# Sigmoid attention and a gated feed-forward layer on one Trainium2 core: output tiles summed in PSUM over three pairs of feed-forward tiles, weight sums rounded on GpSimd, stores issued later, first operands loaded sooner

## The chip, the cores and the metric

The program runs on one core of one Trainium2 chip. The time is that of the device in microseconds (us). The kernel before took 1407.16 us in the median of three runs (1405.22 to 1414.54). Engines are named as in the profile: PE is TensorE (matmul), PEld its weight load, DVE VectorE, ACT ScalarE, POOL GpSimd, and SP SyncE, which here issues every DMA.

## The reference

Twelve heads of 64 in a batch of 8 with 448 positions; the attention's 3584 x 768 output goes through a gated layer with 1536 hidden columns.

```python
scores = scale * np.matmul(q, k.transpose(0, 1, 3, 2)) - np.log(S)
attn = 1.0 / (1.0 + np.exp(-scores))
x = np.matmul(attn, v)                 # then (B*S, H*D) = (3584, 768)
gate = 1.0 / (1.0 + np.exp(-(x @ w_gate)))
val = x @ w_val
return gate * val @ w_out
```

q, k and v are float32; the three weights reach the kernel as 64-bit words, of which VectorE makes two float32 words (hi and lo) by shifts and masks.

## The kernel before, in words

**Stage 1, attention.** 24 steps `m` (8 batches x 3 groups of four heads) of 7 beats `g` each, 168 beats in all. A beat is four matmul calls `scores` (L227), which the profile shows as 8 records, the sigmoid of their result on ACT (L230), and two beats later the `values` matmuls (L244), 8 records too. Score tiles have two buffers in PSUM, so PE's scores wait for ACT's sigmoid of two beats before. When a head pair is done, ACT copies one PSUM half (L254) and DVE adds the other (L261); the sum `x` is stored to DRAM (`xd`).

**The weights.** `Words.first` and `Words.second` (L105 to L125) turn one 128 x 384 chunk of 64-bit words into `t` (hi) and `a`, with eight DVE instructions for a whole chunk (L109 to L112, L122 to L124, L128). `convert` (L130) makes of the chunks what the matmuls need. For a pair `jp` of feed-forward tiles and for gate and value (`t` of the loop), four chunks are a 2 x 2 block; a product of two blocks is made from 7 instead of 8 matmul groups, and for that 7 operands are stored per block: three chunks and four sums of chunks. Each operand is a tile `whl` (hi and lo), stored to `ad` (`store`, L134). The output weights (`wo`, four chunks per pair) are split only and stored to `od` (L169). `convert` is a generator of 32 steps per pair; a chunk takes two steps, a sum one. The weights of the first three pairs (set 0) are converted beside the attention (96 steps over 160 beats), those of the last three (set 1) beside the feed-forward of set 0, where `tick` (L472) advances the generator after every product and every output tile, 96 steps over 280 ticks.

**The pool.** Beside the attention the generator's tiles lie in the pool `att` with two buffers each, beside the feed-forward in `ff` with one buffer each: there `wa` and `wt` of a chunk can be written only when the stores of the chunk before have landed.

**Stage 2, feed-forward.** Eight visits: 2 sets x 4 pairs of batches. In a visit each of three pairs `jp` takes two units of 7 products: gate, then value (`hidden`). A product is 9 matmuls (3 chunks x 3 terms hi and lo, L362) into one of four PSUM banks `un`; ACT or DVE takes it out. A unit's sums run on DVE and two of them on POOL (L373). `hidden` multiplies by the gate and splits the result into `hh` (ACT) and `hl` (DVE). Then come the output tiles: 12 per pair (2 batches x 6 blocks `o`), each 6 matmuls (L442) into one of four banks `mm`, which ACT or DVE adds to a tile `sum` in SBUF (L446, L449, L451). The 36 tiles of a visit stand between its units. The last pair's `sum` goes to DRAM: as `part` in set 0, and as output in set 1, whose first pair adds the loaded `part` (`pb`).

**The next visit's operands.** `load_x` (L176) loads 12 tiles `x`; `split_x` (L183) makes 21 operands `bh`, `bl` of them: 12 subtractions on POOL (L192), 21 roundings on ACT (L196), 21 differences on DVE (L197). For visit 0 this runs beside the attention (from step 8 on), for the others between the last 18 output tiles of a visit, one or two per tile.

**What sets the order.** It is written out by hand: each engine takes its instructions in the order of the program. SP has one queue for all DMAs; an issue that waits holds up those behind it. Operands `A` come through a ring of 7 (`load_operand`, called after each product, waits for that product's matmuls), `wo` through a ring of 8 (`load_out`).

## Time and profile before

| | |
|---|---|
| runs | 1405.22, 1407.16, 1414.54 us |
| the profiled execution | 1409.0 us, its span 1407.2 us |
| busy | PE 1284.3, PEld 1019.8, DVE 840.2, ACT 467.9, POOL 447.6 us |
| mean granted TensorE clock | 0.96 |
| DMA | 341.13 MB, 242 GB/s over the span, 72.2% of 16 engines' time |

Read first which engine the span hangs on, then stage by stage what PE waits for. The busy time of PE counts matmuls that overlap each other and those at a lower clock, so a busy PE is not PE at its peak: the distance from one matmul to the next in a stretch without waits is the measure.

### The profile page before, as it was taken

Reading aid. Unit: us, or ns where it says so; the run is one execution under the profiler, and the core shown is the slowest. Engines: PE = TensorE matmul, PEld = TensorE weight load, DVE = VectorE, ACT = ScalarE, POOL = GpSimd, SP = SyncE. Lnnn points to the kernel's source line nnn. Section 1 sums busy time; section 2 is a strip of 40 time slices with the busy share of each in tenths; the row PEclk is TensorE's granted clock in tenths of the full one; section 3 lists DMA queues with packets and bytes.
Section 4 is the critical chain, followed back from the end, with each engine's and each line's share of the span. In section 5 each row is a group of like instructions: output and inputs, shape, how many; then the busy total and the mean of one; then the engine's idle time right before and its main releaser. Section 6 shows DMA issues by size and latency. Waiting matters only on the chain.

```text
span 1407.2 us, 20966 instructions
## 1 busy us (share of the span) xinstructions
PE 1284.3 (91%) x7456; PEld 1019.8 (72%) x7456; DVE 840.2 (60%) x1466; ACT 467.9 (33%) x769; POOL 447.6 (32%) x388
## 2 busy tenths in 40 slices
PE   8998899979978997799889798999999989989998
PEld 3333333458967986689778796988798878978897
DVE  5575686535678668766785458344734563465445
ACT  6676677732222322222222213212221231122120
POOL 3313523114362344522544124213422332252121
PEclk9999999999999999899989999999899999999999
DMA  8989688878857985596658865875587568747763
GB/s 281 324 279 339 206 311 309 280 271 302 278 183 271 321 281 181 191 359 212 237 195 306 271 194 172 273 255 169 184 292 224 152 207 274 241 124 237 209 194 109
DMA packets 159559, 341.13 MB, mean 242 GB/s; under 512 B 16352, under 2 KB 71776, under 8 KB 159456
## 3 DMA queue, kind: packets, MB, share of 16 engines
q1 hardware_dynamic: 159456, 339.80, 72.2%
q8 instruction: 59, 0.97, 0.3%
q14 instruction: 44, 0.36, 0.1%
HBM read 264.24 MB, written 75.50 MB: 241 GB/s over the span
## 4 chain that ended last, share of the span: by engine, by line
PE 51%; DVE 8%; POOL 8%; DMA 8%; issue 6%; ACT 1%; SPq 0%; POOLq 0%; DVEq 0%; ACTq 0%
PE un L362 35%; PE acc L442 14%; POOL t L192 3%; DMA pb<-part 3%; DVE sum L373 2%; POOL x L192 2%; DVE bl L197 2%; POOL g L418 2%; DMA A<-ad 2%; DMA x<-xd 1%; DMA ad<-whl 1%; PE av L244 1%; POOL c L373 1%; PE sc L227 1%; DMA qk<-qk 1%
## 5 line engine op out<-in xcount | busy, mean ns | idle before, releaser
L362 PE MATMUL un<-bh,A 128*128 128x448 f32 x2016 | 580.0, 367 | 10.4 <-DMA A<-ad 7.6
L442 PE MATMUL acc<-hh,wo 128*128 128x448 f32 x1152 | 370.7, 393 | 85.0 <-DVE sum L373 72.8
L362 PEld LDWEIGHTS un<-bh,A 128*128 128x128 f32 x2016 | 379.5, 188 | 44.5 <-issue 8.3
L362 PE MATMUL un<-bl,A 128*128 128x448 f32 x1008 | 369.4, 367 | 0.0
L442 PEld LDWEIGHTS acc<-hh,wo 128*128 128x128 f32 x1152 | 233.3, 203 | 129.5 <-DVE sum L373 94.3
L373 POOL TENSOR_TENSOR u<-u,p 128x448 f32<-128x448 f32 x48 | 56.4, 1175 | 536.0 <-DVE u L373 536.0
L442 PE MATMUL acc<-hl,wo 128*128 128x448 f32 x576 | 223.3, 388 | 0.0
L362 PEld LDWEIGHTS un<-bl,A 128*128 128x128 f32 x1008 | 189.7, 188 | 16.0
L230 ACT ACTIVATE a<-sc,bias 128x896 f32<-128x896 f32 x168 | 167.9, 1008 | 54.6 <-PE sc L227 52.5
L227 PE MATMUL sc<-qk 64*64 64x448 f32 x1344 | 161.7, 551 | 17.7 <-ACT a L230 17.4
L244 PE MATMUL av<-a,v 64*64 64x448 f32 x1344 | 161.0, 550 | 4.7 <-DMA v<-vv 4.7
L421 ACT CAST hh<-g 128x448 fp32r<-128x448 f32 x96 | 52.7, 566 | 260.9 <-DVE g L418 205.0
L373 DVE TENSOR_TENSOR sum<-acc,sum 128x448 f32<-128x448 f32 x192 | 116.6, 616 | 27.1 <-PE acc L442 26.4
L227 PEld LDWEIGHTS sc<-qk 64*64 64x64 f32 x1344 | 52.0, 137 | 100.4 <-issue 55.0
L442 PEld LDWEIGHTS acc<-hl,wo 128*128 128x128 f32 x576 | 117.3, 204 | 9.2
L244 PEld LDWEIGHTS av<-a,v 64*64 64x64 f32 x1344 | 53.3, 136 | 81.4 <-issue 75.1
L145 POOL CAST whl<-wt 128x384 fp32r<-128x384 f32 x48 | 36.8, 766 | 232.2 <-DVE wt L122 201.7
L407 ACT ACTIVATE g<-c 128x448 f32<-128x448 f32 x96 | 52.1, 573 | 164.1 <-DVE c L373 161.7
L422 DVE TENSOR_TENSOR hl<-g,hh 128x448 fp32r<-128x448 f32 x96 | 65.8, 688 | 62.9 <-ACT hh L421 62.9
L379 ACT COPY p<-un 128x448 f32<-128x448 f32 x48 | 25.4, 530 | 203.6 <-PE un L362 203.6
L159 DVE TENSOR_TENSOR whl<-wf,whl 128x384 fp32r<-128x384 f32 x48 | 33.6, 700 | 99.5 <-ACT whl L158 99.4
L373 DVE TENSOR_TENSOR u<-un,p 128x448 f32<-128x448 f32 x48 | 29.9, 623 | 93.4 <-PE un L362 93.4
(39 smaller groups left out, 1200.9 us busy)
## 6 DMA issues: line engine op xcount, KB each, us to landing
A<-ad SPq DMA_DIRECT2D x336, 384.0 KB, 4.4
wo<-od SPq DMA_DIRECT2D x144, 256.0 KB, 3.7
ad<-whl SPq DMA_DIRECT2D x84, 384.0 KB, 3.0
x<-xd SPq DMA_DIRECT2D x96, 224.0 KB, 5.3
qk<-qk SPq DMA_DIRECT2D x23, 896.0 KB, 6.1
v<-vv SPq DMA_DIRECT2D x24, 448.0 KB, 5.9
xd<-x SPq DMA_DIRECT2D x48, 224.0 KB, 5.8
part<-sum SPq DMA_DIRECT2D x48, 224.0 KB, 2.5
```

The costliest lines, as they stand in the source:

```text
L145: nc.gpsimd.tensor_copy(hl[:, 0], hi)
L159: nc.vector.tensor_tensor(out=hl[:, 1], in0=to, in1=hl[:, 0], op=ALU.subtract)
L192: nc.gpsimd.tensor_tensor(out=xs[to, k], in0=xs[x, k], in1=xs[y, k], op=ALU.subtract)
L227: nc.tensor.matmul(sc[halves[u], h, :S], lhsT=qkt[halves[h], p, k0:k0 + HP], rhs=qkt[halves[h], p, :S], start=True, stop=True)
L230: nc.scalar.activation(a, sc[:, :, :S], AF.Sigmoid, bias=bias, scale=scale)
L244: nc.tensor.matmul(avs[key][halves[h], :S], lhsT=vt[halves[u], g, h], rhs=a[halves[u], h], start=start, stop=g == last)
L362: nc.tensor.matmul(acc, lhsT=w, rhs=m, start=i == 0, stop=i == len(terms) - 1)
L373: engine.tensor_tensor(out=to, in0=x, in1=y, op=ALU.add)
L407: nc.scalar.activation(gates[i], acc, AF.Sigmoid)
L421: nc.scalar.copy(hh, g)
L422: nc.vector.tensor_tensor(out=hl, in0=g, in1=hh, op=ALU.subtract)
L442: nc.tensor.matmul(acc, lhsT=w, rhs=m, start=n == 0, stop=n == len(terms) - 1)
```

## The change

**Output tiles.** A visit runs its six units first and keeps the three pairs' `hh` and `hl` (tags with a slot number). Then it makes 12 output tiles of 18 matmuls, all three pairs accumulated in one PSUM bank (`out_terms`). A tile is taken out once, to `ob`: copied by ACT in set 0, added to `pb` by DVE in set 1. The first two tiles run the terms of pairs 0 and 1 first, and then those of pair 2. The order of the `wo` loads follows (three pairs per `o`). `load_x` and `split_x` of the next visit all lie in this stretch, two steps per tile. In set 1 two `pb` are loaded behind `load_x`, and each next one when its buffer is free. A tile counts as two ticks; the 96 steps of the weights of set 1 are spread over 236 ticks, and a remainder is run after the units of visit 3.

**Rounding.** The rounding of the weight sums moves from ACT to POOL, in both stages (L158 before, L168 after), and so does that of the first `split_x` (L196 before, L213 after, with `cast` given). The DVE difference after a rounding stands one step later.

**Stores.** `store` only notes a store; `send` issues it a step or two later. `whl` has three buffers. The stores of a `wo` chunk are issued (`send(0)`) behind the next chunk's `words.first()`.

**Loads and space.** The ring `A`, the ring `wo` and the sums of a unit move to a pool that lives through both stages; the `x` tiles share the buffers of the sums (`SUMS`). The first 7 `A` are loaded at the start of attention step 23, the first 8 `wo` at the end of the attention.

```diff
         def store(hl, jp, t, n):
-            nc.sync.dma_start(out=a_dram[jp][t][n], in_=hl.bitcast(F32))
+            unsent.append(dict(out=a_dram[jp][t][n], in_=hl.bitcast(F32)))
...
                     words.first()
+                    send(1)
                     yield
+                    send(0)
                     hi, a, e = words.second()
...
-                    nc.scalar.copy(hl[:, 0], to)
+                    nc.gpsimd.tensor_copy(hl[:, 0], to)
+                    yield
                     nc.vector.tensor_tensor(out=hl[:, 1], in0=to, in1=hl[:, 0], op=ALU.subtract)
                     store(hl, jp, t, (1, 2, 3, 5)[n])
-                    yield
             for j in (2 * jp, 2 * jp + 1):
                 for c in range(2):
                     words.first()
+                    send(0)
                     yield
                     hi, a, e = words.second()
                     finish_lo(a.bitcast(F32R), a, e)
                     for n, x in enumerate((hi, a.bitcast(F32))):
-                        nc.sync.dma_start(out=o_dram[jp][c * KC:(c + 1) * KC, :, j % 2, n].rearrange("o p f -> p o f"),
-                                          in_=x.rearrange("p (o f) -> p o f", f=P))
+                        unsent.append(dict(out=o_dram[jp][c * KC:(c + 1) * KC, :, j % 2, n].rearrange("o p f -> p o f"),
+                                           in_=x.rearrange("p (o f) -> p o f", f=P)))
                     yield
+        send(0)
...
-                nc.scalar.copy(hi, x)
+                cast(hi, x)
+                yield
                 nc.vector.tensor_tensor(out=lo, in0=x, in1=hi, op=ALU.subtract)
                 bs[n, k] = hi, lo
-                yield
...
+                if m == B * NQ - 1 and g == 0:
+                    for _ in range(RING):
+                        load_operand()
                 if m == first_x and g == 0:
                     load_x(0)
-                    splits = split_x()
+                    splits = split_x(nc.gpsimd.tensor_copy)
...
+            for slot in range(SET):
+                unit(gate)
+                hs.append(hidden(slot))
...
+            if nxt:
+                load_x(nxt[1])
+                splits = split_x()
+            if last_set:
+                load_part(pr, *tiles[0])
+                load_part(pr, *tiles[1])
...
+                    out_terms(accs[t, o], js, hs, t, o, list(range(SET)))
+                acc = accs.pop((t, o))
+                ob = ff.tile([P, S], F32, tag="ob", name="ob", bufs=2)
+                if s:
+                    plus(ob, acc, pbs.pop((t, o)))
+                    if n + 2 < len(tiles):
+                        load_part(pr, *tiles[n + 2])
+                else:
+                    nc.scalar.copy(ob, acc)
+                b = 2 * pr + t
+                if t == 1:
+                    for _ in range(SET):
+                        load_out()
+                for _ in range(2):
+                    next(splits, None)
+                nc.sync.dma_start(out=out[o, :, b * S:(b + 1) * S] if last_set else part[b][o], in_=ob)
+                tick(2)
```

**Three places in the order.** ACT beside the attention, at about step 10, before (`whl` is a weight sum, `bh` an operand of visit 0, `a` the sigmoid):

```order
L158 CAST whl<-wf 128x384
L196 CAST bh<-x 128x448
L230 ACTIVATE a<-sc,bias 128x896 x2
L254 COPY x<-av 128x448
L158 CAST whl<-wf 128x384
L196 CAST bh<-x 128x448
L230 ACTIVATE a<-sc,bias 128x896 x2
```

The same roundings after stand on POOL, among the weights' own (L154, L157) and the operands' subtractions (L209):

```order
L168 CAST whl<-wf 128x384
L167 TENSOR_TENSOR wf<-wf 128x384
L168 CAST whl<-wf 128x384
L209 TENSOR_TENSOR t<-p_1300,p_1298 128x448
L213 CAST bh<-t 128x448
L209 TENSOR_TENSOR t<-c_1308,u_1306 128x448
L213 CAST bh<-t 128x448
```

ACT's queue there holds only L230 and L254 after the change.

SP's queue in visit 1, where the last `wo` chunks of the fourth pair are stored, before (`wa` and `wt` are the two words of a chunk, `A` the ring's loads, each behind one product):

```order
L169 DMA od3_248<-wt_4844 128x3x128
L169 DMA od3_248<-wa_4843 128x3x128
L336 DMA A_4924<-ad1_0_0_175 128x768
L336 DMA A_4937<-ad1_0_1_176 128x768
L336 DMA A_4950<-ad1_0_2_177 128x768
L102 DMA wraw_4960<-wg 128x384
```

The third and the fourth chunk's stores after, with the chunk loads (`wraw`) that `words.first()` of the following chunk issues:

```order
L139 DMA od3_248<-wt_4780 128x3x128
L139 DMA od3_248<-wa_4779 128x3x128
L227 DMA A_4897<-ad1_0_1_176 128x768
L227 DMA A_4910<-ad1_0_2_177 128x768
L227 DMA A_4924<-ad1_0_3_178 128x768
L227 DMA A_4944<-ad1_0_4_179 128x768
L227 DMA A_4961<-ad1_0_5_180 128x768
L102 DMA wraw_4978<-wg 128x384
L139 DMA od3_248<-wt_4878 128x3x128
L227 DMA A_4992<-ad1_0_6_181 128x768
L227 DMA A_5020<-ad1_1_0_182 128x768
L227 DMA A_5033<-ad1_1_1_183 128x768
```

Before, a chunk's stores stand three loads ahead of the next `wraw`; after, they stand behind it, and the next row there is `od3<-wa_4877`, behind three more `A`.

DVE's queue at the same place after (`c` takes a product out of `un`, `wa_4972` is the next pair's first chunk, whose buffer is that of `wa_4877`):

```order
L393 TENSOR_TENSOR c_4950<-un_4951,u4_4862 128x448
L109 TENSOR_SCALAR wa_4972<-wraw_4883 128x384
L110 TENSOR_SCALAR wa_4972<-wa_4972 128x384
L111 TENSOR_SCALAR wt_4973<-wa_4972 128x384
L112 TENSOR_SCALAR wa_4972<-wa_4972 128x384
L442 TENSOR_TENSOR hl_4966<-g3_4832,hh_4965 128x448
L442 TENSOR_TENSOR hl_4970<-g1_4835,hh_4969 128x448
L393 TENSOR_TENSOR c_4981<-un_4982,u3_4861 128x448
```

Behind the chunk's four instructions on DVE stands the next product's `c`, which frees a PSUM bank.

More of the change, by code (lines that the diff above doesn't have):

```diff
@@ L388, in unit @@
             tick()
-            c = sb("c", bufs=2)
+            c = ff.tile([P, S], F32, tag="c", name="c", bufs=2)
             plus(c, product(4), p1)
@@ L430, in hidden, with out_terms @@
             return hs
-        def out_tile(s, pr, jp, hs, t, o):
-            b = 2 * pr + t
-            first, last = jp == sets[s][0], jp == sets[s][-1]
-            acc = mm.tile([P, 512], F32, tag="mm", name="acc")[:, :S]
+        def out_terms(acc, js, hs, t, o, some):
             terms = []
-            for j in range(2):
-                hh, hl = hs[2 * j + t]
-                w = wos[jp, o][:, j]
-                terms += [(w[:, 1], hh), (w[:, 0], hl), (w[:, 0], hh)]
-            for n, (w, m) in enumerate(terms):
-                nc.tensor.matmul(acc, lhsT=w, rhs=m, start=n == 0, stop=n == len(terms) - 1)
-            if first:
-                sums[t, o] = sb(f"sum{t}{o}")
-                if s:
-                    plus(sums[t, o], acc, pbs.pop((t, o)))
-                    load_part(pr)
-                else:
-                    nc.scalar.copy(sums[t, o], acc)
-            else:
-                plus(sums[t, o], acc, sums[t, o])
-            if t == 1:
-                load_out()
-            if last:
-                to = out[o, :, b * S:(b + 1) * S] if s == len(sets) - 1 else part[b][o]
-                nc.sync.dma_start(out=to, in_=sums[t, o])
-            run_later()
-            tick()
@@ L460, in sigmoid_attention_glu_kernel @@
-        tiles = [(t, o) for t in range(2) for o in range(NO)]
-        parts = []
-        def load_part(pr):
-            if parts:
-                t, o = parts.pop(0)
-                pbs[t, o] = sb("pb", bufs=2)
-                nc.sync.dma_start(out=pbs[t, o], in_=part[2 * pr + t][o])
+            for n in some:
+                for j in range(2):
+                    hh, hl = hs[n][2 * j + t]
+                    w = wos[js[n], o][:, j]
+                    terms += [(w[:, 1], hh), (w[:, 0], hl), (w[:, 0], hh)]
@@ L469, in sigmoid_attention_glu_kernel, with load_part @@
+            for i, (w, m) in enumerate(terms):
+                nc.tensor.matmul(acc, lhsT=w, rhs=m, start=i == 0 and some[0] == 0, stop=i == len(terms) - 1 and some[-1] == SET - 1)
+        pbs = {}
+        def load_part(pr, t, o):
+            pbs[t, o] = ff.tile([P, S], F32, tag="pb", name="pb", bufs=2)
+            nc.sync.dma_start(out=pbs[t, o], in_=part[2 * pr + t][o])
         words = Words(ff, chunks(sets[1]), AHEAD_FF)
-        weights, n_weights, done, ticks, n_ticks = convert(words, sets[1]), 32 * SET, [0], [0], 70 * B // 2
@@ L472, in tick @@
-        def tick():
-            ticks[0] += 1
-            while done[0] < n_weights and done[0] * n_ticks < ticks[0] * n_weights:
+        weights, n_weights, done, ticks, n_ticks = convert(words, sets[1]), 32 * SET, [0], [0], 66 * B // 2 - 28
+        def tick(n=1):
+            ticks[0] += n
+            while done[0] < n_weights - 1 and done[0] * n_ticks < ticks[0] * n_weights:
                 next(weights)
                 done[0] += 1
-        sums = {}
-        for _ in range(RING):
-            load_operand()
```

99 lines of the change are left out of this document (50 added, 49 removed).

## The prediction

> **What bounds the kernel now.** I read first the waits of every engine, since they tell what PE, the busiest engine, waits for (us in total, times, longest):
>
> ```profile
> PE acc L442 <- DVE sum L373: 72.8, 46, 6.4
> PE sc L227 <- ACT a L230: 17.4, 11, 3.1
> PE acc L442 <- ACT sum L449: 11.8, 3, 7.3
> PE un L362 <- DMA A<-ad: 7.6, 1, 7.6
> PE av L244 <- DMA v<-vv: 4.7, 1, 4.7
> ```
>
> Output tiles wait 84.6 us for a PSUM bank, attention 17.4 us for ACT; between the stages lie 7.6 us. Next the chain of waits, for what matmuls take where nothing is waited for, and PE's timeline for the beat, the seam and the end:
>
> ```profile
> 381.16 7.30 PE acc L442 x36
> 441.46 38.30 PE un L362 x189
> ```
>
> ```profile
> 72.24 0.98 PE L227 MATMUL sc<-qk 64*64 64x448 f32 x8 [3.09 <-ACT a L230]
> ...
> 76.99 0.93 PE L227 MATMUL sc<-qk 64*64 64x448 f32 x8
> ...
> 269.75 0.96 PE L227 MATMUL sc<-qk 64*64 64x448 f32 x8
> ...
> 271.25 0.96 PE L227 MATMUL sc<-qk 64*64 64x448 f32 x8
> ...
> 288.54 2.46 PE L244 MATMUL av<-a,v 64*64 64x448 f32 x24
> 298.57 0.71 PE L362 MATMUL un<-bh,A 128*128 128x448 f32 x1 [7.57 <-DMA A<-ad]
> ...
> 1403.61 0.62 DVE L373 TENSOR_TENSOR sum<-acc,sum 128x448 f32<-128x448 f32 x1 [0.59 <-PE acc L442]
> ```
>
> A beat is 1.50 us, so 168 beats are 252 us of the 291.0 us at which the attention ends. A matmul of the feed-forward is 38.30/189 = 0.2026 us. A visit has 6 x 63 + 36 x 6 = 594 of them, 120.4 us; eight are 963 us, yet they take from 298.6 to 1403.6 us, 1105 us. So 142 us are lost there, 84.6 by waits for banks, the rest mostly by a lowered clock after them:
>
> ```profile
> 585.00:728.00 143.00, 127.15 (x590) 114.94 (x591) 100.64 (x177) 39.51 (x77) 57.49 (x48) 0.94 0.75 257
> ```
>
> This is one visit (busy PE, PEld, DVE, ACT, POOL, then the clock, DMA share, GB/s): PE at 0.94 clock, no engine full, DMA at 0.75. The bound is PE with in-order DVE and ACT queues that come late to its banks. What a wait does to the clock stands in the timeline: from 72.24 to 76.99 lie four groups of 8, 4.75 us instead of 4 x 0.75, so a wait of 3.09 us costs another 1.75 us.
>
> **Attention.** Why ACT is late there, from its waits up to 292 us:
>
> ```profile
> ACT bh L196 <- POOL t L192: 11.1, 4, 3.4
> ACT whl L158 <- DMA ad<-whl: 8.2, 5, 4.2
> ACT whl L158 <- POOL wf L157: 5.7, 5, 3.3
> ACT bh L196 <- POOL x L192: 3.0, 1, 3.0
> ```
>
> All of it, 28 us, is rounding that stands ahead of a sigmoid in ACT's queue. The change moves every such rounding to POOL. Of PE's 17.4 us about 0.8 us (first beat, small ones) stay: 16.6 us go. Of the 291 us, 291 - 252 - 17.4 - 4.7 = 17 us are start and low clock; of the latter I take 7 us away, since the 4.7 us wait for `v` behind 12 `x` issues stays, and with it its own slow stretch. POOL pays for it:
>
> ```profile
> 0.00:291.00 291.00, 267.20 (x2704) 106.08 (x2704) 186.27 (x382) 206.28 (x261) 81.25 (x88) 0.97 0.82 283
> L145 POOL CAST whl<-wt 128x384 fp32r<-128x384 f32 x48 | 36.8, 766 | 232.2 <-DVE wt L122 201.7
> ```
>
> 24 roundings of 0.77 us and 21 of 448 columns, by that row an estimate of 0.77 x 448/384 = 0.89 us, add 37 us to POOL's 81 us: 118 of some 270 us. The Trainium skill, page "GPSIMD Engine Reference", section "Key points", states that GpSimd shares its SBUF interfaces with VectorE and contends with its instructions of two SBUF inputs; by it the 37 us could hold up DVE for as long, an estimate, and the trace agrees in kind (606 to 1582 ns, row in the last rival). POOL isn't full, but where sums of weights and operand splits meet, POOL falls behind, DVE then waits for it, and DVE frees the `values` banks, which have four beats (6 us) of slack. No row shows POOL so loaded; the cost lies between 0 and the 16.6 us that the same work cost in ACT's queue. I take 2 us, near the low end, because DVE's difference now stands one step later. A gain isn't possible there beyond the waits counted. The same 283 GB/s x 291 us move in less time (some 310 GB/s); I take 2 us for that. Attention ends at 291.0 - 16.6 - 7 + 4 = 271.4 us.
>
> **The seam.** The first 7 `A` are issued at the start of the last step, 10 us ahead, and their buffers wait for nothing: of 7.6 us 0.2 remain. The feed-forward starts at 271.6 us. The 8 `wo` have 77 us of units in front of them and cost nothing.
>
> **Output tiles.** What 18 matmuls in one bank remove, and what loads stand around them:
>
> ```profile
> L373 DVE TENSOR_TENSOR sum<-acc,sum 128x448 f32<-128x448 f32 x192 | 116.6, 616 | 27.1 <-PE acc L442 26.4
> x<-xd SPq DMA_DIRECT2D x96, 224.0 KB, 5.3
> wo<-od SPq DMA_DIRECT2D x144, 256.0 KB, 3.7
> pb<-part SPq DMA_DIRECT2D x48, 224.0 KB, 3.4
> 613.94 8.07 SPq L180 DMA_DIRECT2D x<-xd  x12
> 1184.89 6.70 DMA pb<-part
> ```
>
> 192 sums go, 117 us of DVE. A bank is now needed every 18 x 0.2026 = 3.65 us instead of 1.22, and with four banks the take-out may be 7 to 11 us late before PE stops. What stands between two take-outs in a queue (two `bl` on DVE, two roundings on ACT, near 0.6 us each) is far shorter. So the 84.6 us of waits go, and the low clock that followed. What is late next are the loads, since SP issues them in order. Let T be the end of the units. One `A` and 12 `x` are issued until T+9 (8.07 us for the 12). In set 1 come two `pb`, landing 3.4 to 6.7 us later, T+13 to T+16; the take-out of tile 0 is over at T+16.7 at the latest, while PE has filled four banks at T+14.6: 0 to 2 us. Behind the take-outs stand three `wo`; the ninth, needed in tile 4 after its first 12 matmuls (T+14.6+2.4 = T+17 or, held by the bank, T+19), is issued at T+17 and lands at T+20.8: 1.8 us. Each later round trip (3.4 us, or 6.7 at the worst, and 0.6 us of DVE) fits in the 7.3 us of two tiles. I take 3.8 us, for the late `pb`, in each of the three visits of set 1 that load `x`: 11.4 us. The last visit loads none. In set 0 the take-out is ACT's copy and needs no load; the ninth `wo` is issued at T+10 and is in time. There I take 2.5 us a visit, 10 us, for the first tiles' wait for the last `hl` behind the weights' work on DVE (PE has 24 matmuls, 4.9 us, as cover).
>
> **Stores issued later.** For `whl`, with three buffers, a store goes one step (some 4.5 us in the units, 2.46 ticks) before its buffer is needed; it hides. For `wo` chunks it is the other way. `words.first()` of the next chunk writes the only `wa`, so it must wait for the stores, and these now are issued at the same place of the program, not a step earlier. Before, in visit 2 of set 0, when SP happened to be late there:
>
> ```profile
> 624.74 0.37 SPq L169 DMA_DIRECT2D od<-wa  x1
> ...
> 630.52 0.36 DVE L109 TENSOR_SCALAR wa<-wraw 128x384 uint32<-128x384 uint32 x1 [4.78 <-DMA od<-wa]
> ```
>
> ```profile
> DVE wa L109 <- DMA od<-wa: 25.4, 7, 7.0
> od<-wa SPq DMA_DIRECT2D x24, 192.0 KB, 3.9
> ```
>
> The first row is DVE's from 298 to 862 us, all of set 0. After, 11 such waits stand in the chunks of set 1 (4 per pair; the last pair's last has none behind it). SP reaches the store some 1.2 to 1.6 us after product k (an `A`, a `wraw`, two stores at 0.4 us); it lands 3.9 to 5.8 us later; four DVE instructions of 0.4 us and the first take-out of 0.6 us follow: PE gets a bank 7.2 to 9.5 us after product k. With four banks it runs 4 x 1.82 = 7.3 us. By the order, five of the waits have DVE take-outs right behind them: 0 to 2.2, I take 1.1 us each, 5.5 us. Four cost nothing: one lies among output tiles, three have products that ACT takes out behind them. Two are worse: at a pair's end `send(1)` keeps back one store, which SP then issues three products after the DVE wait in one case and two in the other. DVE is free 3 x 1.82 + 0.8 + 3.9 (to 5.8) + 2.1 = 12.3 to 14.2 us after product k, PE stands 5 to 6.9 us, say 6.0; the other, with 1.82 less, 4.2 us. Each is long enough for the slow clock, 1.9 us each by the 1.75 us above. Sum 5.5 + 10.2 + 3.8 = 19.5 us, all of it new.
>
> **The sum.** 271.6 + 963.2 + 19.5 + 10 + 11.4, and after the last matmul the take-out, store and end, as before 1407.2 - 1403.6 = 3.6: 1279 us of span. The profiled execution was 1.8 us above its span and 1.8 us above the median, so the number is 1279 us. Its unknown parts (POOL 0 to 16, chunk waits 5 to 30, loads 0 to 20) give 1262 to 1298.
>
> **The rivals.** *The loads and stores fit better* (chance 0.14): SP runs late anyway, DVE reaches `words.first()` later still and finds the stores landed. For it speaks that only 7 such waits show before. 15 us of the chunk waits, 10 of the loads, 8 of set 0 go: 1246 us.
>
> *The tile stretch is bound by DMA* (0.13). 12 `x`, 18 `wo`, 12 `pb` and 12 results are 13.0 MB in 43.8 us, 296 GB/s; the visit above had 257 on average. If the stretch got only that, it would take 50.5 us or more, 7 us in each visit: 1279 + 8 x 7 - 6 = 1329 us. Against it:
>
> ```profile
> 300.00:320.00 20.00, 20.00 (x94) 18.12 (x93) 9.93 (x18) 4.34 (x8) 6.14 (x7) 0.95 1.02 383
> ```
>
> 383 GB/s were moved here, with PE busy; at that rate the stretch's 13.0 MB take 34 of 43.8 us. The Trainium skill, page "DMA: Bandwidth & Descriptors", section "Where 436 GB/s comes from", gives 358 GB/s as HBM's limit for one core; by it the estimate is 36 us, and the trace's window lies above that figure.
>
> *GpSimd takes ACT's place in the attention* (0.09): POOL's queue, itself waiting for stores of `whl`, holds DVE, DVE the banks: 16.6 us and 5 us of low clock come back, 1301 us. For it speaks that POOL waited 17.8 us for `whl` stores before:
>
> ```profile
> POOL whl L145 <- DMA ad<-whl: 17.8, 3, 8.5
> ```
>
> Against it, those came with two buffers, now three.
>
> *DVE is stretched by POOL* (0.06, half of it slower than before, half within 1%). DVE's differences of two SBUF operands vary (ns, least/median/most):
>
> ```profile
> L197 DVE TENSOR_TENSOR bl<-x,bh x96: 606/618/1582, 111.6 to 1274.2; 128x448 fp32r<-128x448 f32 x96
> ```
>
> A factor of 2.6, where POOL runs beside. In set 0 DVE has 100.6 us in a visit, without 24 sums of 0.616 us 85.9 of 120.4 us. Stretched by 1.4, DVE would be the bound there, and from 1.78 on (152 us), (1407 - 1279)/4 = 32 us a visit, the gain is gone; at the 2.6 of the row a visit would take 223 us, and the whole 1279 + 4 x 103 = 1690 us. Against it, the median lies by the least although POOL was busy 40% of the visit above, and only 24 x 0.77/4, some 5 us of POOL, are added per visit.
>
> **How the numbers follow.** The forecast has 0.58. Ends for 8 in 10: 1246 (half of the first rival beyond) to 1329 (half of the second beyond), with the last outside: 0.07 + 0.06 + 0.06 are left out. About 1% is what a measurement of this kernel can tell from none. Faster by more: 0.58 + 0.14 + 0.13 + 0.09 = 0.94; 0.03 within; 0.03 slower.
>
> **What would show it.** Attention: PE's waits for ACT near 1 us, its last `values` near 271 us, and no gap before the first L385. Units of 38.3 us per 189 matmuls but for set 0, where the longest PE waits must stand behind the first chunk of the fifth and the sixth pair, 4 to 7 us. Waits of the output tiles for `ob` below 25 us. It is wrong if PE's waits in tile stretches reach 40 us, if DMA's share there is at 1, or if POOL or DVE are above 95% busy over whole visits.

## The result and the profile after

The changed kernel takes 1328.69 us in the median of four runs (1323.23 to 1333.29), the kernel before 1408.67 us beside it: a ratio of 0.943, 95% interval 0.938 to 0.948. It is 80 us faster; the prediction said 1279 us, which would have been 130 us, and the time lies at the very upper end of its range (1329 us). The profiled execution took 1328.5 us, its span is 1326.7 us. Medians here and below are over fast runs: one run of all the experiments, 1399.31 us at a granted clock of 0.845, was slow and is left out.

First the waits of PE in the kernel after (us in total, times, longest):

```profile
PE un L385 <- DVE c L393: 19.3, 9, 5.5
PE acc L460 <- DMA wo<-od: 13.9, 6, 4.0
PE av L280 <- DVE x L297: 13.3, 10, 2.3
PE un L385 <- DVE u L393: 13.2, 7, 4.2
PE un L385 <- issue: 3.7, 1, 3.7
...
PE acc L460 <- DVE ob L393: 0.6, 1, 0.6
...
PE sc L263 <- ACT a L266: 0.4, 1, 0.4
```

The 84.6 us that output tiles waited for banks are 0.6 us, and the 17.4 us for ACT's sigmoid are 0.4 us. New are 32.5 us of products that wait for a bank (`un`, two rows), 13.9 us for `wo`, 13.3 us of the attention for DVE's `x`. PE's timeline at the seam shows no gap, and the chain of waits shows the last visit:

```profile
276.70 2.63 PE L280 MATMUL av<-a,v 64*64 64x448 f32 x22
...
279.26 0.47 PE L385 MATMUL un<-bh,A 128*128 128x448 f32 x1
```

```profile
821.94 72.97 PE un L385 x360
...
1202.55 76.60 PE un L385 x378
1279.15 43.79 PE acc L460 x216
```

The last visit has 594 matmuls in 120.4 us with nothing waited for, as predicted. So the loss can be laid out by stage against the prediction's own terms. The attention ends at 279.3 us instead of 271.6 (7.7 us over). Set 0 lasts from 279.3 to 821.9 us, 61.1 us above four such visits; predicted were 29.5 (31.6 over). Set 1 with the end lasts 504.8 us, 23.2 us above four visits; predicted were 15.0 (8.2 over). That is 47.5 of the 47.7 us by which the span misses 1279. The worst visit is the third of set 0 (143.9 us; its row leaves out the two ends), the best the last (us, busy PE, PEld, DVE, ACT, POOL, then clock, DMA share, GB/s):

```profile
550.00:692.00 142.00, 127.48 (x586) 113.91 (x585) 92.03 (x151) 36.55 (x72) 64.44 (x59) 0.94 0.77 261
...
1203.00:1323.00 120.00, 119.93 (x592) 110.81 (x590) 39.78 (x65) 19.11 (x36) 21.61 (x18) 1.00 0.66 202
```

The worst visit is as long, and at the same clock, as the same visit before, the one of 143 us that the prediction quotes. In this visit the waits for banks were given back in full as other waits.

### The profile page after: what moved, and what is told of

It reads as the page before. It is cut to its first block, busy times and chain, and to the rows that moved or that the text cites. A ratio compares the mean times of both kernels' runs of the same rounds, so it can differ in the third digit from the quotient of the medians.

```text
span 1326.7 us, 20773 instructions
## 1 busy us (share of the span) xinstructions
PE 1253.1 (94%) x7456; PEld 1029.1 (78%) x7456; DVE 757.0 (57%) x1274; ACT 440.4 (33%) x700; POOL 483.2 (36%) x457
## 4 chain that ended last, share of the span: by engine, by line
PE 61%; DVE 14%; DMA 11%; POOL 5%; issue 4%; SPq 2%; ACT 2%; DVEq 0%; POOLq 0%; ACTq 0%
PE un L385 34%; PE acc L460 14%; PE av L280 7%; PE sc L263 7%; DMA od<-wa 4%; DVE bl L215 2%; DMA wo<-od 2%; DVE c L393 1%; DMA ad<-whl 1%; DMA pb<-part 1%; DMA c<-xd 1%; POOL g L438 1%; DVE wa L109 1%; DVE wa L110 1%; DVE wt L122 1%
## 5 line engine op out<-in xcount | busy, mean ns | idle before, releaser
L460 PE MATMUL acc<-hh,wo 128*128 128x448 f32 x1152 | 334.1, 369 | 15.0 <-DMA wo<-od 13.9
L460 PEld LDWEIGHTS acc<-hh,wo 128*128 128x128 f32 x1152 | 218.1, 189 | 36.9 <-DMA wo<-od 16.5
L280 PE MATMUL av<-a,v 64*64 64x448 f32 x1344 | 211.3, 540 | 16.0 <-DVE x L297 13.3
L263 PE MATMUL sc<-qk 64*64 64x448 f32 x1344 | 211.0, 542 | 0.4 <-ACT a L266 0.4
L280 PEld LDWEIGHTS av<-a,v 64*64 64x64 f32 x1344 | 73.6, 134 | 78.8 <-issue 45.8
L263 PEld LDWEIGHTS sc<-qk 64*64 64x64 f32 x1344 | 73.1, 134 | 70.0 <-issue 52.2
L393 DVE TENSOR_TENSOR ob<-acc,pb 128x448 f32<-128x448 f32 x48 | 29.8, 622 | 121.4 <-DMA y<-ob 78.4
L154 POOL CAST whl<-wt 128x384 fp32r<-128x384 f32 x48 | 37.5, 780 | 166.6 <-DVE wt L122 166.6
L438 POOL TENSOR_TENSOR g<-c,g 128x448 f32<-128x448 f32 x48 | 63.9, 1332 | 66.2 <-DVE c L393 63.6
L109 DVE TENSOR_SCALAR wa<-wraw 128x384 uint32<-128x384 uint32 x72 | 39.8, 552 | 80.2 <-DMA od<-wa 60.8
L393 DVE TENSOR_TENSOR c<-un,u 128x448 f32<-128x448 f32 x96 | 59.0, 618 | 31.2 <-PE un L385 29.8
```

What stands on the lines that cost most here:

```text
L109: nc.vector.tensor_scalar(out=a, in0=raw[:, :, 1], scalar1=0x7FFFFFFF, scalar2=None, op0=ALU.bitwise_and)
L154: nc.gpsimd.tensor_copy(hl[:, 0], hi)
L263: nc.tensor.matmul(sc[halves[u], h, :S], lhsT=qkt[halves[h], p, k0:k0 + HP], rhs=qkt[halves[h], p, :S], start=True, stop=True)
L280: nc.tensor.matmul(avs[key][halves[h], :S], lhsT=vt[halves[u], g, h], rhs=a[halves[u], h], start=start, stop=g == last)
L393: engine.tensor_tensor(out=to, in0=x, in1=y, op=ALU.add)
L438: engine.tensor_tensor(out=g, in0=acc, in1=g, op=ALU.mult)
```

## The experiments

Each was run beside the kernel before; times are medians of four runs (of two or three, where said). The medians of before were 1405.75 to 1409.41 us; ratios are to those.

### How much the single accumulation gives: three groups of six

The units still come first, but a tile's 18 matmuls are three groups in three banks, each taken out and added in SBUF. The first two tiles no longer run the terms of pairs 0 and 1 ahead of those of pair 2.

```diff
-                    accs[t, o] = mm.tile([P, 512], F32, tag="mm", name="acc")[:, :S]
-                    out_terms(accs[t, o], js, hs, t, o, list(range(SET)))
...
+                for k in range(SET):
+                    acc = mm.tile([P, 512], F32, tag="mm", name="acc")[:, :S]
+                    out_terms(acc, js, hs, t, o, [k])
...
+                    if k:
+                        plus(ob, acc, ob)
+                    elif s:
+                        plus(ob, acc, pbs.pop((t, o)))
...
+                    else:
+                        nc.scalar.copy(ob, acc)
```

> Each output tile as three groups of 6 matmuls again, each taken out by itself and added in SBUF on DVE, in the changed kernel's order (units first, tiles after). Theory: the single accumulation is what frees the tile stretch; with three take-outs DVE has in set 0 some 49 us of work in a stretch of 43.8 us, in set 1 some 39 us, in order behind differences that wait for ACT and POOL, and PE waits for banks again: 40 to 60 us slower than 1328.7, so 1369 to 1389 us. Rival: the new order of the tiles and of split_x is what removed the waits, and the take-outs matter little: within 15 us of 1328.7.

It took 1386.76 us (1379.12 to 1392.15), ratio 0.985 (0.979 to 0.992): 58 us of the gain hang on this edit. PE's two longest groups of waits in it:

```profile
PE acc L460 <- DVE ob L393: 26.4, 12, 6.9
PE acc L460 <- ACT hh L441: 15.5, 8, 2.9
```

The wait for DVE's take-out is back (ACT's take-outs add 10.3 us), since a bank is needed every six matmuls again. The second row is another matter: it comes once per visit, at the first tile's terms of the last pair, and was 0.5 us in the kernel after. So the 58 us belong to the single accumulation and to the order of the first two tiles together; this run doesn't part them.

### The new waits of set 0: stores at once, or two buffers

The theory: DVE stands at `words.first()` until the late stores of the chunk before have landed, and the take-outs behind it in DVE's queue come late. Two runs remove the cause in two ways. The first issues a `wo` chunk's stores where they are made:

```diff
                                            in_=x.rearrange("p (o f) -> p o f", f=P)))
+                    send(0)
                     yield
```

> The stores of a wo chunk go at once again (send(0) behind them), all else as in the changed kernel, which took 1328.7 us; its profile has 32.5 us of PE waiting for DVE between products of set 0, and about 12 us of low clock behind the longest of these. Theory: these waits come from the stores, which are issued beside the next chunk's words.first() and so hold DVE for their landing. Then the store has a step of 4.5 us as a lead, PE's waits in the units fall below 12 us, and the time by 25 to 40 us, to about 1290 to 1303 us. Rival: DVE has too much of the weights' work per tick (0.41 steps instead of 0.34); then the waits stay above 20 us and the time within 8 us of 1328.7.

The second leaves the stores late and gives `wa` and `wt` two buffers:

```diff
-            a = self.pool.tile([P, CW], U32, tag="wa", name="wa")
-            t = self.pool.tile([P, CW], U32, tag="wt", name="wt")
+            a = self.pool.tile([P, CW], U32, tag="wa", name="wa", bufs=2)
+            t = self.pool.tile([P, CW], U32, tag="wt", name="wt", bufs=2)
```

> Two buffers for wa and wt beside the feed-forward, the stores as late as in the changed kernel. Theory of the store wait: DVE never waits for od stores in the units of set 0, PE's waits there fall below 8 us, 1283 to 1298 us, a few us below the kernel with stores at once. Rival, too much DVE work per tick: within 8 us of 1328.7, with PE still waiting over 20 us there.

They took 1298.59 us (ratio 0.923, 0.920 to 0.927) and 1292.08 us (0.918, 0.914 to 0.922), 30 and 36.6 us below the kernel after. PE's waits for a bank of products, of the first and of the second run:

```profile
PE un L386 <- DVE c L394: 6.8, 6, 1.8
PE un L386 <- DVE u L394: 3.9, 3, 2.4
```

```profile
PE un L385 <- DVE u L393: 1.3, 2, 1.0
PE un L385 <- DVE c L393: 1.1, 4, 0.4
```

32.5 us became 10.7 and 2.4 us. The store is the cause. One reason why it cost more than predicted is in DVE's timeline of the kernel after, at the fourth pair, and in PE's:

```profile
418.79 0.36 DVE L109 TENSOR_SCALAR wa<-wraw 128x384 uint32<-128x384 uint32 x1 [4.94 <-DMA od<-wa]
...
422.05 0.62 DVE L393 TENSOR_TENSOR u<-un,p 128x448 f32<-128x448 f32 x1
426.61 0.36 DVE L109 TENSOR_SCALAR wa<-wraw 128x384 uint32<-128x384 uint32 x1 [3.95 <-DMA od<-wa]
```

```profile
422.72 0.47 PE L385 MATMUL un<-bh,A 128*128 128x448 f32 x1 [1.68 <-DVE u L393]
...
428.74 0.74 PE L385 MATMUL un<-bh,A 128*128 128x448 f32 x1 [3.93 <-DVE u L393]
...
456.18 0.74 PE L385 MATMUL un<-bh,A 128*128 128x448 f32 x1 [5.47 <-DVE c L393]
...
581.46 0.74 PE L385 MATMUL un<-bh,A 128*128 128x448 f32 x1 [4.83 <-DVE c L393]
...
623.03 0.50 PE L385 MATMUL un<-bh,A 128*128 128x448 f32 x1 [4.41 <-DVE c L393]
```

Between these two waits for stores DVE does the eight word instructions of one chunk and a single take-out, then waits again. PE enters the second wait with its banks full: DVE stands from 422.66 us, PE already from 428.74 - 3.93 = 424.81 us, 2.2 us later, where the prediction gave every wait four free banks, 7.3 us.

### The waits for wo in set 1: pb first

```diff
+            if last_set:
+                load_part(pr, *tiles[0])
+                load_part(pr, *tiles[1])
             splits = iter(())
             if nxt:
                 load_x(nxt[1])
                 splits = split_x()
-            if last_set:
-                load_part(pr, *tiles[0])
-                load_part(pr, *tiles[1])
```

> In set 1 the two loads of pb stand ahead of the twelve loads of x of the next visit instead of behind them. Theory (the late pb holds the first take-out, that holds the third wo issue, PE waits for wo): PE's waits for wo, 13.9 us in six, fall below 5 us, the three visits of set 1 that load x take 121 to 124 us instead of 125 to 129, 6 to 14 us in all, 1314 to 1323 us. Rival (the wo are late since the tile stretch's transfers fill the DMA engines): waits for wo stay above 10 us whatever goes first, 1324 to 1332 us.

It took 1309.72 us (1306.39 to 1317.89), ratio 0.931 (0.927 to 0.935), 19 us below the kernel after, more than the 6 to 14 us expected. SP's timeline of the first visit of set 1, in the kernel after with the wait of PE, then in this run:

```profile
906.57 6.44 SPq L466 DMA_DIRECT2D pb<-part  x3
...
914.17 1.39 SPq L235 DMA_DIRECT2D wo<-od  x3
...
919.58 0.47 PE L460 MATMUL acc<-hh,wo 128*128 128x448 f32 x1 [4.01 <-DMA wo<-od]
```

```profile
896.02 0.90 SPq L466 DMA_DIRECT2D pb<-part  x2
...
906.33 1.52 SPq L235 DMA_DIRECT2D wo<-od  x3
```

After, the third `pb` waits in SP's queue until the first take-out has freed its buffer, and that take-out waits for the late first `pb`; the three `wo` stand behind. Loaded first, `pb` doesn't hold the queue, and the `wo` go 10.7 instead of 15.6 us after the end of the visit's units, 4.9 us earlier (set 1 began 2.9 us earlier in this run, which is the rest of what the two rows differ by). In set 1 PE has then no wait at all in the trace. The rival (transfers fill the engines) falls: the same bytes move.

### The head of the feed-forward: wo later

```diff
-        for _ in range(RING_OUT):
-            load_out()
...
         tiles = [(t, o) for o in range(NO) for t in range(2)]
+        for _ in range(RING_OUT):
+            load_out()
```

> The first eight loads of wo stand behind the first chunk loads of the feed-forward's weights in SP's queue instead of ahead of them; nothing else moves. Theory (DVE at the head of the feed-forward waits for a chunk that lands behind eight wo, and the first product's take-outs stand behind DVE's wait): PE's waits of 3.7 and 1.1 us at 294 to 298 us go, with the slow stretch behind them, and the wo are needed only 77 us later; 4 to 7 us off, 1321 to 1325 us. Rival (chunk and wo share the same bandwidth, the chunk isn't earlier): DVE's wait for wraw stays above 8 us and the time at 1326 to 1332 us.

It took 1319.56 us (1315.45 to 1326.19), ratio 0.937 (0.933 to 0.940). The interval touches that of the kernel after, so the traces have to decide. PE's and DVE's timeline after, and DVE's in this run:

```profile
294.20 0.45 PE L385 MATMUL un<-bh,A 128*128 128x448 f32 x1 [3.73 <-issue]
...
297.75 0.74 PE L385 MATMUL un<-bh,A 128*128 128x448 f32 x1 [1.07 <-DVE u L393]
```

```profile
292.02 0.36 DVE L109 TENSOR_SCALAR wa<-wraw 128x384 uint32<-128x384 uint32 x1 [11.56 <-DMA wraw<-wg]
```

```profile
285.29 0.36 DVE L109 TENSOR_SCALAR wa<-wraw 128x384 uint32<-128x384 uint32 x1 [5.10 <-DMA wraw<-wg]
```

DVE's first chunk comes 6.7 us earlier, both waits of PE go (0.9 us is left), and set 0 ends at 814.1 instead of 821.9 us. This is a wait that the prediction didn't have: it said that the 8 `wo` "cost nothing", looking at PE alone and not at the chunk load behind them in SP's queue.

### The attention: three tries on the 13.3 us for DVE's x

The first gives the 21 operand roundings of visit 0 back to ACT, the second the weight sums' roundings.

```diff
-                    splits = split_x(nc.gpsimd.tensor_copy)
+                    splits = split_x()
```

> The rounding of visit 0's operands beside the attention on ACT again, the weight sums' rounding still on GpSimd. In the changed kernel PE waits 13.3 us for the values banks, behind DVE's x, and the attention ends at 279.3 us. Theory: it is these 21 roundings on GpSimd, with the subtractions there, that hold DVE; then the 13.3 us fall below 4 us, PE waits 6 to 11 us for ACT instead, and the attention ends between 272 and 280 us; the time stays within 7 us of 1328.7. Rival: the weight sums' rounding holds DVE; then the 13.3 us stay, the waits for ACT come on top, and the attention ends 6 to 12 us later.

```diff
-                    nc.gpsimd.tensor_copy(hl[:, 0], to)
+                    nc.scalar.copy(hl[:, 0], to)
```

> The rounding of the 48 weight sums goes back to ACT in both stages; visit 0's operand roundings stay on POOL. Theory (in the attention either engine's queue costs about the same, as with the operands' roundings): POOL loses some 37 us, PE's waits for DVE's x fall from 13.3 to below 8 us, PE's waits for ACT's sigmoid rise from 0.4 to 4 to 12 us, the attention ends within 4 us of 279.3; in the feed-forward nothing changes; 1322 to 1333 us. Rival (POOL's load stretches DVE in the whole of set 0 and makes the chunk waits longer): DVE's busy time falls by over 20 us and the visits of set 0 get shorter by 3 us each, below 1316 us.

They took 1327.08 us (0.944, 0.940 to 0.949) and 1335.88 us (three runs; 0.947, 0.943 to 0.950). Neither can be told from the kernel after by its time. The traces tell more: the first product of the feed-forward starts at 280.0 us in the first and at 288.7 us in the second, against 279.3 us after. PE's largest wait of the attention, in the first run and in the second:

```profile
PE sc L263 <- ACT a L266: 15.2, 5, 6.1
```

```profile
PE sc L263 <- ACT a L266: 15.2, 6, 6.2
```

With either group back on ACT, ACT is late again, and PE's waits for DVE's `x` all but go. For the operands that is an even trade, for the weight sums a loss of 9 us in the attention and nothing in the feed-forward (set 0 takes 541.3 instead of 542.5 us). My expectation for the second (the end within 4 us) was wrong: by these traces the move of the sums to POOL is worth 9 of the 12 us by which the attention became shorter. PE's named waits explain only 2 of the 9 us; the attention's mean granted clock is 0.96 instead of 0.99.

The third try does the operands two per step instead of three, so that POOL and DVE are less full from 120 to 200 us:

```diff
-                if m > first_x and g % 2:
+                if m > first_x and g in (1, 4):
```

> Visit 0's operand splits go two per attention step (beats 1 and 4) instead of three, and so last until about step 19 instead of 16; the work is the same. Theory (while three splits per step run, POOL and DVE are near full from 120 to 200 us, DVE comes late to the values' banks): PE's waits for DVE's x, 13.3 us in ten, fall below 5 us, the attention ends at 268 to 275 instead of 279.3 us, the time is 1316 to 1325 us. Rival (what holds DVE is the weights' own chain, DVE waiting for POOL's whl, at any pace of the splits): the waits stay at 10 us or more, only later, and the time stays at 1325 to 1332 us.

It took 1327.72 us (0.942, 0.939 to 0.945): nothing. PE's waits for `x` are 11.3 us, now in five, the attention ends where it did, and the theory fell. The rival's numbers came true, and the trace has what it named: DVE waits for POOL's `whl` three times from 146 to 156 us, 6.1 us in all. Something else shows in DVE's timeline just ahead of PE's longest wait in it (5.65 us at 169.38 us), and in POOL's beside it:

```profile
161.54 1.18 DVE L111 TENSOR_SCALAR wt<-wa 128x384 uint32<-128x384 uint32 x1
...
163.26 1.48 DVE L122 SCALAR_TENSOR_TENSOR wt<-wraw,wt 128x384 uint32<-128x384 uint32 x1
...
168.03 0.36 DVE L111 TENSOR_SCALAR wt<-wa 128x384 uint32<-128x384 uint32 x1
...
169.24 0.55 DVE L122 SCALAR_TENSOR_TENSOR wt<-wraw,wt 128x384 uint32<-128x384 uint32 x1
```

```profile
161.25 1.24 POOL L209 TENSOR_TENSOR c<-g,c 128x448 f32<-128x448 f32 x1
...
163.09 1.24 POOL L209 TENSOR_TENSOR g<-x,g 128x448 f32<-128x448 f32 x1
```

POOL's last instruction there ends at 166 us. While it ran, DVE's instructions took 1.18 and 1.48 us; without it the same lines take 0.36 and 0.55 us. The long ones end soon after the POOL instruction beside them: at 162.72 us behind 162.49, and at 164.74 behind 164.33. In these two rows DVE's instruction ends 0.2 and 0.4 us behind POOL's, whatever it takes by itself. So a new theory: POOL stretches DVE while it runs, whatever the pace. It was tried on both sides.

### Is it POOL? Roundings that nothing needs

A new tile `scr`, which nothing reads, is rounded into once per beat in six steps of the attention.

```diff
+                if 2 <= m < 8:
+                    nc.gpsimd.tensor_copy(scr, zeros)
```

> The kernel after with 42 more roundings of 128x448 on POOL, one per beat in steps 2 to 7 of the attention (21 to 84 us), into a tile that nothing reads; no other engine has more to do. Theory (POOL running beside it stretches DVE's instructions whose operands all lie in SBUF, with one input or two; not those that read PSUM): DVE's busy time from 20 to 80 us, 43.0 us in the kernel after, rises by 6 to 16 us, L111 and L112 (one input, 0.36 us) and L122 (0.55 us) among them, L297 (which reads PSUM) stays at 0.62 us. Rival (the long DVE instructions of 120 to 200 us come from the DMA's share or from the operands' places, not from POOL): DVE's busy time rises by less than 3 us. A narrower rule (only two SBUF inputs are held up): L111 and L112 stay at 0.36 us. The time as a whole within 10 us of the kernel after.

It took 1332.47 us (two runs). In DVE's busy time the expectation missed: 44.27 us from 20 to 80 us instead of 42.97, which is the rival's bound (less than 3 us more), not 6 us; but it is for 75 instructions instead of 85, since the weights also ran behind, so the sum decides nothing. By instruction (ns, least/median/most; the window's groups by line), after and then in this run:

```profile
L111 DVE TENSOR_SCALAR wt<-wa x8: 359/360/361, 23.6 to 78.4; 128x384 uint32<-128x384 uint32 x8
```

```profile
L111 DVE TENSOR_SCALAR wt<-wa x7: 361/525/596, 23.7 to 78.5; 128x384 uint32<-128x384 uint32 x7
...
L297 DVE TENSOR_TENSOR x<-av,x x11: 607/611/618, 21.8 to 79.6; 128x448 f32<-128x448 f32 x11
```

L111, with one input, goes from 0.36 to up to 0.60 us beside a rounding; L297, one of whose two inputs lies in PSUM, doesn't move. L122 with two SBUF inputs went from 0.549 to 0.599 us in the mean (most of its seven had no dummy beside them), and L170 from 0.950 to 0.877. DMA's share in the window is lower than after (0.89 instead of 0.96), so it isn't the reason. So POOL does stretch DVE, and not only where both inputs lie in SBUF. PE feels it: up to 90 us it waits 3.3 us, in four, for DVE's `x`, where the kernel after has no such wait. But DVE's waits for POOL's `whl` rose there too, from 10.9 to 14.6 us, so this run doesn't say how much of the 3.3 us is the stretch. The rule that the prediction quotes of the Trainium skill, page "GPSIMD Engine Reference", section "Key points", names two SBUF inputs, and also instructions in a mode with two ports; whether L111 runs in such a mode no run here shows.

### Three edits together, and ACT a step behind POOL

The same three diffs as above, the core of them:

```diff
+            a = self.pool.tile([P, CW], U32, tag="wa", name="wa", bufs=2)
+            t = self.pool.tile([P, CW], U32, tag="wt", name="wt", bufs=2)
...
         tiles = [(t, o) for o in range(NO) for t in range(2)]
+        for _ in range(RING_OUT):
+            load_out()
...
+            if last_set:
+                load_part(pr, *tiles[0])
+                load_part(pr, *tiles[1])
             splits = iter(())
```

> Three of the edits together: two buffers for wa and wt, the first eight wo behind the chunk loads, the two pb ahead of the loads of x. Theory (the three causes are separate waits, so their gains add): 36.6 + 9.1 + 19.0 us off 1328.7 is 1264 us, range 1256 to 1274; PE's waits in the feed-forward below 6 us in all; what is left above eight visits of 120.4 us is the attention to 279 us, 3.6 us of end and under 20 us. Rival (they relieve the same SP queue and overlap): 1280 us or more.

It took 1264.93 us (1263.07 to 1272.01), ratio 0.901 (0.898 to 0.904). The three gains add to within 1 us. PE's waits in it, and the chain through a visit of set 1:

```profile
PE av L280 <- DVE x L297: 12.3, 9, 2.3
PE acc L458 <- DMA wo<-od: 3.3, 2, 3.1
```

```profile
775.80 76.61 PE un L383 x378
852.40 43.78 PE acc L458 x216
```

All four visits of set 1 take 120.4 us. Set 0 takes 496.1 us, 14.5 above four visits, with 6.7 us of named waits, a little above the 6 expected; what the rest is stays open.

The last run adds, beside the attention, visit 0's roundings on ACT, but a step behind POOL's subtraction:

```diff
-    def split_x(cast=nc.scalar.copy):
+    def split_x(cast=nc.scalar.copy, ahead=False):
...
                     nc.gpsimd.tensor_tensor(out=xs[to, k], in0=xs[x, k], in1=xs[y, k], op=ALU.subtract)
+                    if ahead:
+                        yield
...
-                    splits = split_x(nc.gpsimd.tensor_copy)
+                    splits = split_x(ahead=True)
```

> As the three edits together, and beside the attention the 21 operand roundings of visit 0 go back to ACT, each a step behind the subtraction on POOL that makes its operand, so that ACT doesn't wait for POOL. Theory (ACT was late through POOL's lateness, not through the rounding's own 0.6 us; DVE through POOL running beside it): neither wait is left, PE's waits for ACT's a and for DVE's x are below 6 us together, the attention ends at 266 to 274 instead of 279 us, and the time is 5 to 13 us below that of the three edits. Rival (ACT has no room for 0.6 us beside a sigmoid per beat): PE's waits for ACT stay above 10 us, the attention ends at 278 us or later.

It took 1259.77 us (1253.92 to 1267.21), ratio 0.897 (0.892 to 0.901), the lowest of all, though its interval overlaps that of the three edits. PE's wait for ACT and the first product:

```profile
PE sc L265 <- ACT a L268: 7.9, 4, 3.2
```

```profile
271.78 0.47 PE L385 MATMUL un<-bh,A 128*128 128x448 f32 x1
```

The attention ends 7.9 us earlier than with the three edits (279.7 us), at the 271.4 us that the prediction had. PE's waits for ACT and `x` are 8.3 us together, not below 6: ACT still waits for POOL's subtractions, by the same trace 11.4 us in five. Of the 7.9 us, 4.8 are left in the span; where set 0 gives back the rest wasn't followed up.

### The seam undone

```diff
-                if m == B * NQ - 1 and g == 0:
-                    for _ in range(RING):
-                        load_operand()
...
+        for _ in range(RING):
+            load_operand()
```

> The first seven loads of A stand at the end of the attention again, not at the start of its last step. Theory (the seam is the wait for the first A): PE's first product of the feed-forward waits 6 to 8 us for A and some slow-clock time follows, 6 to 11 us in all, 1334 to 1340 us. Rival (the loads issued in the last step delay others by as much as they save): 1325 to 1332 us.

It took 1333.03 us (1327.71 to 1340.23), ratio 0.949 (0.945 to 0.952), 4.3 us above the kernel after, which the intervals can't tell from none, and between the ranges of the theory and its rival. PE's timeline has the wait:

```profile
283.98 0.71 PE L384 MATMUL un<-bh,A 128*128 128x448 f32 x1 [6.30 <-DMA A<-ad]
```

It starts 4.7 us later than after, though the attention itself ended 1.6 us earlier; the wait at the head of the feed-forward is then smaller by 2 us. So the early `A` are worth 6.3 us where they stand (7.4 were predicted), and what they are worth to the whole, 4 us by the medians, isn't clear of the noise.

## Why the prediction was right, and where it was wrong

**What bounds it, and the output tiles: right.** Waits for banks in tiles fell from 84.6 to 0.6 us, the visits without other trouble take 120.4 us, and the groups of six, with the first tiles' order, put 58 us back.

**The seam: right.** 0.2 us were to remain; the first product follows the last `values` without a gap.

**The attention: the wait right, POOL's price wrong.** PE's waits for ACT fell to 0.4 us (about 1 was said). But "I take 2 us, near the low end" for POOL was 13.3 us of waits for `x`, within the bounds of 0 to 16.6 us; the end came 7.7 us late, though POOL's busy time rose by 27.6 and not by 37 us. The failed step is the guess that POOL costs only when DVE waits for it, and then little. That wait is there: in the attention DVE waits 28.7 us for POOL's `whl` (45.5 us for ACT's before), and 1.98 us of it stand ahead of PE's longest wait for `x`, 2.30 us. But from 122 to 149 us DVE waits for nothing, and four of the ten waits, 5.6 us, lie there: ahead of them stand only DVE's own instructions, stretched beside POOL (up to 1.29 us for L109, which takes 0.36 us alone). One more, 1.30 us, stands behind a `wo` store that came late (2.78 us of DVE). How the rest divides stays open. The last rival had the stretch, but put it in the feed-forward. In set 0 there is little more of it than before: DVE's operand differences take 0.88 us in the mean, 0.85 us before, and giving the sums' roundings back to ACT left set 0 as long as it was.

**Stores of the wo chunks: the mechanism and the two long waits right, the sum too small.** Predicted were 6.0 and 4.2 us behind the pair ends; measured are 5.47 and 4.41 us. The failed step is "five of the waits [...] I take 1.1 us each" and "Four cost nothing": the other waits of PE above 0.9 us in set 0, without those at its head, are 1.68, 3.93, 0.99, 4.83, 4.22, 1.69, 1.65 and 1.25 us, 20.2 instead of 5.5 us. Each wait was priced alone with four free banks. For 3.93 and 4.22 us the banks were nearly full when DVE came to stand: PE stood 2.2 us later both times. For 4.83 us PE had its four banks, but the store took long to land, as SP's and DVE's timeline shows:

```profile
571.72 0.37 SPq L139 DMA_DIRECT2D od<-wa  x1
...
579.32 0.36 DVE L109 TENSOR_SCALAR wa<-wraw 128x384 uint32<-128x384 uint32 x1 [9.33 <-DMA od<-wa]
```

That is 7.6 us, where 3.9 to 5.8 were allowed. The 1.65 and 1.25 us have no store wait right ahead of them; DVE was still behind from the one before. The term was 19.5 us; taking its cause away gave 36.6 us.

**Set 0's other 10 us: half of the story missing.** The wait for the first chunk behind eight `wo` wasn't in it; moving the `wo` gave 9.1 us by the medians, 7.8 us by set 0's end in the traces.

**Set 1's loads: the waits right, their aftermath forgotten.** 11.4 us were predicted, and PE waits there 11.5 us for `wo`. But the three visits lost 19.4 us (126.7, 128.8 and 125.1 us), and `pb` first gave back 19.0. The slow clock after a wait, 1.75 us by the prediction's own row, was added to the chunk waits and not to these. The chain of waits has it behind the first of them:

```profile
919.58 29.05 PE acc L460 x132
```

At 0.2026 us each the 132 matmuls would take 26.7 us; the granted clock is 0.61 for the first 4.4 us. Behind the second long wait it is much the same (28.58 us), behind the third, of 2.67 us, the clock stays at 1.00. That is some 4 of the 7.9 us between waits and loss; the rest has no name in the trace. Why the `wo` came so late was half right: in the visit shown among the experiments the units end at T = 898.6 us, SP reached the `wo` at T+15.6 (T+17 was said), and they took 919.6 - 914.2 = 5.4 us to land, not 3.8.

**The rivals.** That the tile stretch is bound by DMA gave 1329 us, the measured time almost to the digit, and is nonetheless wrong: in the last visit and in all of set 1 with `pb` first the tiles run at full pace. A right number is no evidence for its mechanism. That the time lies inside the stated range is luck too: its upper end came from this rival, while the parts that did go over, by their own bounds, ended at 1298 us. That loads and stores fit better was wrong in its sign.

The terms as measured nearly close the account: 36.6 (stores), 19.0 (`pb`) and 9.1 (head) were predicted as 19.5, 11.4 and 0, 33.8 us more; the attention adds 7.7. That is 41.5 of the 47.7 us. Another 4.5 us are the rest of set 0 (14.5 us with the three edits, 10 predicted), whose cause stays open.

## What to carry to other kernels

A wait in an in-order queue is priced with the slack that is left when it comes, not with all of it: waits that follow each other closely share one set of free buffers, and here eight that were to cost 5.5 us cost 20 us, in part for this reason. When a transfer is moved, look at what stands behind it in the issuing queue for every engine, since a load that PE needs late can hold one that DVE needs now. Moving elementwise work to GpSimd relieved its old engine here, but part of it was paid in VectorE's time: price both the waits for GpSimd and the stretch of what runs beside it.

## What the runs showed of the hardware that was not expected

Landing times of some transfers grew, and that hits each wait for one. DMA issues of the kernel after, median us from issue to landing at the end of the row:

```profile
wo<-od SPq DMA_DIRECT2D x144, 256.0 KB, 4.9
...
y<-ob SPq DMA_DIRECT2D x48, 224.0 KB, 5.2
```

`wo` took 3.7 us before, the results' stores 2.0 us, while the loads of `A`, the most of all, fell from 4.4 to 3.9 us. The mean traffic rose from 242 to 257 GB/s; whether that or the closer order of these transfers is the reason, no run here shows. The results' stores are at 5.2 us in the run with the three edits too, where PE doesn't wait for them.

A DVE instruction of 128x448 with an input in PSUM took 0.61 to 0.63 us throughout the kernel after, whether POOL worked beside it or not, where one of the same size within SBUF took 0.61 to 1.58 us in the row that the prediction quotes of before. The take-outs of the banks thus were never slowed themselves; they came late because of what stood ahead of them in DVE's queue.
